# Tile loads of an attention stage: the two heads of a pair on alternate partitions instead of on two halves

## The chip, the core and the metric

The kernel runs on one core of one Trainium2 chip. The metric is the device time of one execution in microseconds. The kernel before took 518.98 us (median of three runs: 518.98, 525.2, 514.63); its profiled execution took 520.31 us, of which the profile's span covers 518.5 us.

## The reference

Attention over chunks, followed by a mixture of experts to which tokens are assigned greedily by gate score with a capacity:

```python
# attention: q, k, v (4, 8, 768, 64), mem_k, mem_v (4, 8, 8, 64)
for c in range(24):                       # chunks of 32 queries
    k_full = concat([mem_k, k[left 16 .. own 32 .. right 8]])   # up to 64 keys
    scores = (q_c @ k_full^T) / 8
    a = softmax(scores)                   # maximum subtracted, sum + 1e-9
    out_c = a @ v_full
# experts: x = attention's output as (3072, 512)
logits = x @ w_gate                       # (3072, 8)
# pairs (token, expert) in falling order of logit; a token takes the first
# expert that has room, each expert takes 384 tokens
for e in range(8):
    h = relu(x[mask_e] @ w1[e])           # (384, 1024)
    out[mask_e] = h @ w2[e]               # (384, 512)
```

All inputs and outputs are float32.

## The kernel before

**Stages.** First comes attention, then the routing of the first expert, then the eight experts with their products, with the routing and the weight preparation of later experts woven in. The change touches attention and one helper that prepares constants.

**Tiles of attention.** The work is cut into 24 tiles. A tile holds one batch, four chunks of 32 queries, and all 8 heads. The heads go in four pairs. A matmul contracts over 128 partitions, and two heads of 64 dimensions share them: the queries `q` of a tile have both heads of a pair stacked over the partitions, and the keys are stored as two blocks, one of which is zero where the other head's dimensions lie. So one matmul with the keys of both blocks gives the scores of both heads, with no mixing. The same trick is used for the values: `s["v"]` are blocks with data on one head's partitions and zeros on the other's.

**The buffers.** Five buffers `kvb` (`NB`) of 128 partitions rotate over the tiles. The columns of each are, in order, `o0`, `v0`, `k0`, `q`, `k1`, `v1`, `o1`, `end` (class `LAY`): odd-chunk values, even-chunk values and keys of head 0, the queries of both, then keys and values of head 1. In the kernel before, head 0 of a pair lies on partitions 0 to 63 and head 1 on 64 to 127. The zero blocks are written once at the start (L69 to L75), since the loads never write to them: data and zeros lie on different partitions.

**The loads.** `load(i)` issues a tile's transfers on SP's queue. The values of even and odd chunks share their first 32 of 64 rows; these rows are loaded once (`cut`) and copied on the chip by `shared(i)`: on GpSimd for head 0 (L128) and on ScalarE for head 1 (L129). Tile 0 is loaded in six transfers, every other tile in four.

**The order of work.** It is written out by hand: in step `t` of a loop over tiles the list `steps` (L231) calls `scores(t)`, `softmax(t)`, `shared(t-1)`, `ptrans(t-1)`, `xtrans(t-3)`, `av(t-2)`, `norm(t-2)`, `rows(t-3)`, `logits2(t-5)` and `logits(t-4)`, and then `load(t+3)`. Each engine takes its instructions in this order. `scores` is 16 matmuls into PSUM (four column groups of 32 at a time); `softmax` is a maximum and a subtraction on VectorE and an exponential on ScalarE; `ptrans` transposes the weights on TensorE; `av` is the product with the values; `rows` scales a tile's rows on GpSimd and stores them to the scratch tensor `xs` in DRAM, through buffers `xr`. `load(t+3)` writes the buffer that `av(t-2)` has read, and SP waits for that.

**Constants.** The generator `constants` (L733) is advanced one step at each tile from the fifth on. Its first step issues the load of the table `cc` on ScalarE's queue and, right behind, casts on GpSimd that read it; later steps fill the tile `io` piece by piece.

Of the kernel before, what the change touches and what calls it, by code (L numbers as in the profile page):

```python
# [11 lines left out]
F32 = mybir.dt.float32  # L12
# [48 lines left out]
def attention(g):  # L61
# [6 lines left out]
    nc.vector.memset(g.zero, 0.0)  # L68
    for i in range(NB):  # L69

        (nc.vector if i < 3 else nc.gpsimd).memset(kvb[i][0:64, L.q + DM:], 0.0)
        if i % 2 == 0:
            nc.scalar.activation(kvb[i][64:P, 0:L.q], g.zero[64:P].to_broadcast([64, L.q]), AF.Copy)
        else:
            nc.gpsimd.memset(kvb[i][64:P, 0:L.q], 0.0)  # L75
    make_identity(nc, g.ident)
# [6 lines left out]

    def load(i):
        kv = kvb[i % NB]

        full = slice(0, L.q + DM), slice(L.q, L.end)
        cut = slice(L.v0, L.q + DM), slice(L.q, L.o1)
        if i == 0:
            first = slice(L.k0, L.q + DM), slice(L.q, L.v1)  # L90
            own = slice(L.v0, L.k0), slice(L.v1, L.o1)
            parts = (0, 64, first), (0, 64, own), (32, 64, (slice(0, L.v0), slice(L.o1, L.end)))
        else:
            parts = (0, 32, cut), (32, 64, full)
        for r0, r1, part in parts:
            for hf, c in enumerate(part):
                r = slice(64 * hf + r0, 64 * hf + r1)
                nc.sync.dma_start(kv[r, c], g.kv[i, r, c.start - L.q * hf:c.stop - L.q * hf])
        st[i] = dict(q=kv[:, L.q:L.q + DM].rearrange("p (r c n) -> p r c n", r=4, c=4), kv=kv,
                     k=blocks(kv, L.k0, L.k1, KW).rearrange("p a (m t n) -> p a m t n", t=3, n=32),  # L100
                     v=[blocks(kv, a, b, VW).rearrange("p a (m n) -> p a m n", n=D + 1)
                        for a, b in ((L.v0, L.v1), (L.o0, L.o1))])

    def scores(i):
        s = st[i]
        ps = pp.tile([P, H, NK], F32, tag="A", name="ps_s")
        for pr in range(4):
            for c in range(4):
                o = ps[32 * c:32 * c + 32, 2 * pr:2 * pr + 2, :]
                nc.tensor.matmul(o.rearrange("p a (t n) -> p a t n", t=2),  # L110
                                 s["q"][:, pr, c, :], s["k"][:, :, 2 * pr + c // 2, 0:2 + c % 2:1 + c % 2],
                                 start=True, stop=True, tile_position=(0, 32 * c))
        s["s"] = ps

    def softmax(i):
        s = st[i]
        ps = s["s"]
        mx = ab.tile([P, H], F32, tag="mx", name="mx", bufs=2)
        nc.vector.tensor_reduce(mx, ps, axis=AX.X, op=ALU.max)
        sub = ab.tile([P, H, NK], F32, tag="sub", name="sub", bufs=2)  # L120
        nc.vector.tensor_tensor(sub, ps, mx.unsqueeze(2).to_broadcast([P, H, NK]), op=ALU.subtract)  # L121
        pe = ab.tile([P, H * NK], F32, tag="pexp", name="pexp", bufs=2)
        nc.scalar.activation(pe, sub.rearrange("p h n -> p (h n)"), AF.Exp, scale=scale)  # L123
        s["p"] = pe

    def shared(i):
        kv = st[i]["kv"]
        nc.gpsimd.tensor_copy(kv[0:32, L.o0:L.v0], kv[0:32, L.v0:L.k0])  # L128
        nc.scalar.activation(kv[64:96, L.o1:L.end], kv[64:96, L.v1:L.o1], AF.Copy)  # L129

# [47 lines left out]
    def rows(i):  # L178
        s = st[i]
        finish(s["pow2"])  # L180
        sx = s["pr"]
        xr = ab.tile([P, XW], F32, tag="xr", name="xr", bufs=2)
        nc.gpsimd.tensor_tensor(xr[:, 0:DM], s["x"], sx[:, 0].to_broadcast([P, DM]), op=ALU.mult)  # L183
        nc.gpsimd.tensor_copy(xr[:, DM:DM + 1], sx[:, 1])
        nc.gpsimd.dma_start(g.xs[i * P:(i + 1) * P, 0:DM + 1], xr[:, 0:DM + 1])
# [42 lines left out]
    def keys(i):  # L228
        finish(first_keys(g, i - 3, i + 1))

    steps = [(scores, 0), (softmax, 0), (shared, 1), (ptrans, 1), (xtrans, 3), (av, 2), (norm, 2), (rows, 3),  # L231
             (logits2, 5), (logits, 4)]
    n = NT - 1
    for t in range(n):
# [6 lines left out]
        yield  # L241
    for f, i in ((scores, n), (shared, n - 1), (ptrans, n - 1), (softmax, n), (shared, n), (xtrans, n - 3),
                 (av, n - 2), (ptrans, n), (logits, n - 4), (rows, n - 3), (av, n - 1), (av, n), (logits2, n - 4),
                 (early, 0), (xtrans, n - 2), (logits, n - 3), (xtrans, n - 1), (logits, n - 2), (early, 1),
                 (xtrans, n), (logits, n - 1), (logits, n), (early, 2), (logits2, n), (hist, 0), (keys, n)):
        f(i)
# [486 lines left out]
def constants(g, consts):  # L733
# [239 lines left out]
def layout(q, k, v, mem_k, mem_v, moe_w_gate, moe_w1, moe_w2):  # L973
# [11 lines left out]
    def order(outside):  # L985
# [38 lines left out]
```

## Time and profile before

| | |
|---|---|
| median of three runs | 518.98 us |
| profiled execution | 520.31 us |
| span of its profile | 518.5 us |
| TensorE busy | 424.6 us (82%) |
| VectorE busy | 315.2 us (61%) |
| ScalarE busy | 329.8 us (64%) |
| GpSimd busy | 253.8 us (49%) |
| first score matmul, last tile's score matmuls | 6.31 us, 121.01 us |
| moved by DMA | 78.87 MB, mean 152 GB/s |

How to read it: busy times are of instructions on the engine; "waited for" tells what ended an idle time; the DMA share is the mean busy share of the core's 16 DMA engines; the clock is the share of TensorE's full clock that was granted. In rows of waits the columns are the total in microseconds, the number of times, and the longest. The page's slices are 13 us wide, so the first nine cover attention.

### The profile page before, as it was taken

Reading aid. Unit: us, or ns where it says so; the run is one execution under the profiler, and the core shown is the slowest. Engines: PE = TensorE matmul, PEld = TensorE weight load, DVE = VectorE, ACT = ScalarE, POOL = GpSimd, SP = SyncE. Lnnn points to the kernel's source line nnn. Section 1 sums busy time; section 2 is a strip of 40 time slices with the busy share of each in tenths; the row PEclk is TensorE's granted clock in tenths of the full one; section 3 lists DMA queues with packets and bytes.
Section 4 is the critical chain, followed back from the end, with each engine's and each line's share of the span. In section 5 each row is a group of like instructions: output and inputs, shape, how many; then the busy total and the mean of one; then the engine's idle time right before and its main releaser. Section 6 shows DMA issues by size and latency. Waiting matters only on the chain.

```text
span 518.5 us, 11009 instructions
## 1 busy us (share of the span) xinstructions
PE 424.6 (82%) x4140; PEld 259.9 (50%) x4140; DVE 315.2 (61%) x1140; ACT 329.8 (64%) x515; POOL 253.8 (49%) x264
## 2 busy tenths in 40 slices
PE   2669677888334686988999999999999999999993
PEld 1447556667232453444555555555555555654641
DVE  4445554655878376775787777787787876423220
ACT  5546664766303857566789578668858956999810
POOL 6145554555122504425638536735825814965821
PEclk9988997999756698697999999999999999999998
DMA  8989999992018200910371290091083069611001
GB/s 214 244 205 272 275 277 267 260 315 101 0 63 296 90 2 1 367 59 21 125 283 41 61 346 20 26 368 55 22 291 136 22 213 362 199 61 40 21 22 40
DMA packets 20150, 78.87 MB, mean 152 GB/s; under 512 B 3776, under 2 KB 3904, under 8 KB 18624
## 3 DMA queue, kind: packets, MB, share of 16 engines
q1 hardware_dynamic: 14048, 58.88, 36.8%
q0 software_dynamic: 5760, 18.90, 10.1%
q8 instruction: 33, 0.54, 0.4%
q10 hardware_dynamic: 288, 0.37, 0.3%
q14 instruction: 21, 0.17, 0.1%
HBM read 65.54 MB, written 12.60 MB: 151 GB/s over the span
## 4 chain that ended last, share of the span: by engine, by line
PE 52%; DVE 16%; DMA 14%; ACT 8%; issue 6%; POOL 2%; SPq 1%; POOLq 0%; DVEq 0%; ACTq 0%
PE ps_hid L684 19%; PE ps_y L703 18%; DMA kvb<-in_kv_dram 13%; PE D L513 3%; PE D L365 2%; PE ps_xg L660 2%; PE ps_av L150 2%; PE ps_s L110 2%; DMA cc<-in_consts_dram 2%; DVE hl L692 2%; ACT hh L691 2%; DVE oa L352 1%; ACT xh L663 1%; DVE xl L666 1%; ACT w1f L602 1%
## 5 line engine op out<-in xcount | busy, mean ns | idle before, releaser
L605 POOL TENSOR_TENSOR w2l<-w2f,w2h 128x1024 f16<-128x1024 f32 x32 | 67.9, 2130 | 35.7 <-ACT w2h L604 35.7
L605 POOL TENSOR_TENSOR w1l<-w1f,w1h 128x1024 f16<-128x1024 f32 (+1 forms) x33 | 68.3, 2075 | 28.7 <-ACT w1h L604 22.4
L684 PEld LDWEIGHTS <-w1h 128*128 128x128 f16 x512 | 48.0, 99 | 33.2 <-issue 4.8
L692 DVE SCALAR_TENSOR_TENSOR hl<-ps_hid,hh 128x384 f16<-128x384 f32 x64 | 35.1, 555 | 42.3 <-ACT hh L691 41.5
L590 POOL DMA_INDIRECT xg<-xs,ids x24 | 23.0, 960 | 72.8 <-DVE R L310 35.7
L703 PEld LDWEIGHTS <-hh 128*128 128x128 f16 x384 | 36.4, 99 | 41.4 <-issue 4.2
L691 ACT ACTIVATE hh<-ps_hid 128x384 f16<-128x384 f32 x64 | 31.1, 486 | 41.0 <-PE ps_hid L684 40.9
L684 PE MATMUL ps_hid<-xh,w1h 128*128 128x384 f16 x256 | 53.5, 332 | 2.4 <-ACT xh L663 2.4
L615 ACT ACTIVATE jk<-w1f 128x1024 f16<-128x1024 f32 x32 | 33.8, 1056 | 33.0 <-DMA w1f<-in_w_dram 31.8
L110 PE MATMUL ps_s<-kvb 128*32 128x128 f32 x768 | 29.3, 293 | 30.8 <-DMA kvb<-in_kv_dram 28.1
L183 POOL TENSOR_TENSOR xr<-x,sxp 128x512 f32<-128x512 f32 x24 | 24.9, 1036 | 59.6 <-DVE sxp L549 23.4
L684 PE MATMUL ps_hid<-xl,w1h 128*128 128x384 f16 x256 | 53.6, 333 | 0.0
L684 PE MATMUL ps_hid<-xh,w1l 128*128 128x384 f16 x256 | 53.1, 331 | 0.0
L703 PE MATMUL ps_y<-w2h,hh 128*128 128x512 f16 x192 | 47.7, 386 | 3.5 <-ACT w2h L604 3.5
L703 PE MATMUL ps_y<-w2h,hl 128*128 128x512 f16 x192 | 50.5, 389 | 0.0
L703 PE MATMUL ps_y<-w2l,hh 128*128 128x512 f16 x192 | 49.7, 389 | 0.0
L716 POOL DMA_INDIRECT out_dram<-y,ids x24 | 23.8, 994 | 43.0 <-DVE y L709 31.2
L123 ACT ACTIVATE pexp<-sub 128x512 f32<-128x512 f32 x24 | 15.1, 630 | 42.2 <-DVE sub L121 42.2
L110 PEld LDWEIGHTS ps_s<-kvb 128*32 128x32 f32 x768 | 22.6, 117 | 34.8 <-issue 34.4
L602 ACT ACTIVATE w1f<-w1f,s1s 128x1024 f32<-128x1024 f32 (+1 forms) x33 | 36.8, 1114 | 0.9 <-ACT s1s L566 0.4
L615 ACT ACTIVATE jk<-w2f 128x1024 f16<-128x1024 f32 x32 | 33.8, 1056 | 5.0 <-DMA w2f<-in_w_dram 2.7
L602 ACT ACTIVATE w2f<-w2f,s2s 128x1024 f32<-128x1024 f32 x32 | 36.5, 1139 | 0.0
(174 smaller groups left out, 855.5 us busy)
## 6 DMA issues: line engine op xcount, KB each, us to landing
w1f<-in_w_dram SPq DMA_DIRECT2D x32, 512.0 KB, 5.7
w2f<-in_w_dram SPq DMA_DIRECT2D x32, 512.0 KB, 8.3
kvb<-in_kv_dram SPq DMA_DIRECT2D x46, 290.0 KB, 8.3
kvb<-in_kv_dram SPq DMA_DIRECT2D x46, 225.0 KB, 7.1
xs<-xr POOLq DMA_DIRECT2D x24, 256.5 KB, 7.5
kvb<-in_kv_dram SPq DMA_DIRECT2D x2, 320.0 KB, 4.4
xg<-xs,ids POOLq DMA_INDIRECT x24, 5.3
out_dram<-y,ids POOLq DMA_INDIRECT x24, 2.8
```

The lines of the kernel that those rows point to most:

```text
L110: nc.tensor.matmul(o.rearrange("p a (t n) -> p a t n", t=2), s["q"][:, pr, c, :], s["k"][:, :, 2 * pr + c // 2, 0:2 + c % 2:1 + c % 2], st ...
L183: nc.gpsimd.tensor_tensor(xr[:, 0:DM], s["x"], sx[:, 0].to_broadcast([P, DM]), op=ALU.mult)
L513: nc.tensor.matmul(ps4, oh[:, :, i], ri[:, i].rearrange("p a b -> p (a b)"), start=(i == 0), stop=(i == NT - 1))
L590: nc.gpsimd.indirect_dma_start(out=xg[a], out_offset=None, in_=g.xs, in_offset=bass.IndirectOffsetOnAxis(ap=ids[:, a:a + 1], axis=0))
L602: nc.scalar.activation(f, f, AF.Copy, scale=s[:, 0:1])
L605: nc.gpsimd.tensor_tensor(l, f, h, op=ALU.subtract)
L615: g.nc.scalar.activation(jk, st[k]["f" + n][j], AF.Abs, accum_out=am[:, j:j + 1])
L684: nc.tensor.matmul(ph[:, 0:CAP], w[:, f // 2, kc, (f % 2) * P:(f % 2) * P + P], x[:, kc, :], start=(n == 0), stop=(n == 3 * KC - 1))
L691: nc.scalar.activation(hh[:, f], ph[:, 0:CAP], AF.Relu)
L692: nc.vector.scalar_tensor_tensor(hl[:, f], ph[:, 0:CAP], 0.0, hh[:, f], op0=ALU.max, op1=ALU.subtract)
L703: nc.tensor.matmul(py, h[:, f, t], w[:, f, :], start=(n == 0), stop=(n == 3 * FC - 1))
L716: sc = g.nc.gpsimd.indirect_dma_start(out=g.out, in_=y, in_offset=None, out_offset=bass.IndirectOffsetOnAxis(ap=ids, axis=0))
```

## The change

The data in DRAM and in the buffers are put in another order. Head 0 of a pair takes the even partitions and head 1 the odd ones, so a tile's transfer for one head goes to 64 partitions with a step of 2 (`kv[hf:P:2, c]`). A tile is loaded in two transfers of 64 rows, tile 0 in four. The rows that even and odd chunks share are stored and loaded twice; `shared` is gone. [...] Scores are written with the two heads alternating, (key, head) instead of (head, key), so that transposed weights have the heads on alternate partitions as well; the matmul's output and the maximum's input have a step of two words. `constants` pauses for five tiles after it has issued the load of the table and three fills, and only then uses the table. `xr` has three buffers instead of two.

```diff
-    for i in range(NB):
-        (nc.vector if i < 3 else nc.gpsimd).memset(kvb[i][0:64, L.q + DM:], 0.0)
-        if i % 2 == 0:
-            nc.scalar.activation(kvb[i][64:P, 0:L.q], g.zero[64:P].to_broadcast([64, L.q]), AF.Copy)
-        else:
-            nc.gpsimd.memset(kvb[i][64:P, 0:L.q], 0.0)
+    nc.gpsimd.memset(kvb[0][:, L.k1:L.v1], 0.0)
+    nc.vector.memset(kvb[0][:, L.k0:L.q], 0.0)
+    nc.vector.memset(kvb[0][:, 0:L.k0], 0.0)
+    nc.gpsimd.memset(kvb[0][:, L.v1:L.end], 0.0)
+    for i in range(1, NB):
+        for r, e in ((slice(0, L.q), i), (slice(L.k1, L.end), i + 1)):
+            if e % 3 == 1:
+                nc.scalar.activation(kvb[i][:, r], g.zero.to_broadcast([P, L.q]), AF.Copy)
+            else:
+                (nc.vector if e % 3 == 0 else nc.gpsimd).memset(kvb[i][:, r], 0.0)
...
     def load(i):
         kv = kvb[i % NB]
-        full = slice(0, L.q + DM), slice(L.q, L.end)
-        cut = slice(L.v0, L.q + DM), slice(L.q, L.o1)
+        parts = [(slice(0, L.k1), slice(L.q, L.end))]
         if i == 0:
-            first = slice(L.k0, L.q + DM), slice(L.q, L.v1)
-            own = slice(L.v0, L.k0), slice(L.v1, L.o1)
-            parts = (0, 64, first), (0, 64, own), (32, 64, (slice(0, L.v0), slice(L.o1, L.end)))
-        else:
-            parts = (0, 32, cut), (32, 64, full)
-        for r0, r1, part in parts:
+            parts = [(slice(L.k0, L.k1), slice(L.q, L.v1)), (slice(0, L.k0), slice(L.v1, L.end))]
+        for part in parts:
             for hf, c in enumerate(part):
-                r = slice(64 * hf + r0, 64 * hf + r1)
-                nc.sync.dma_start(kv[r, c], g.kv[i, r, c.start - L.q * hf:c.stop - L.q * hf])
+                nc.sync.dma_start(kv[hf:P:2, c], g.kv[i, hf, :, c.start - L.q * hf:c.stop - L.q * hf])
...
-        ps = pp.tile([P, H, NK], F32, tag="A", name="ps_s")
+        ps = pp.tile([P, 4, NK, 2], F32, tag="A", name="ps_s")
         for pr in range(4):
             for c in range(4):
-                o = ps[32 * c:32 * c + 32, 2 * pr:2 * pr + 2, :]
-                nc.tensor.matmul(o.rearrange("p a (t n) -> p a t n", t=2),
-                                 s["q"][:, pr, c, :], s["k"][:, :, 2 * pr + c // 2, 0:2 + c % 2:1 + c % 2],
+                o = ps[32 * c:32 * c + 32, pr].rearrange("p (t n) a -> p a t n", t=2)
+                nc.tensor.matmul(o, s["q"][:, pr, c, :], s["k"][:, :, 2 * pr + c // 2, 0:2 + c % 2:1 + c % 2],
                                  start=True, stop=True, tile_position=(0, 32 * c))
...
-        nc.vector.tensor_reduce(mx, ps, axis=AX.X, op=ALU.max)
+        nc.vector.tensor_reduce(mx, ps.rearrange("p r n a -> p r a n"), axis=AX.X, op=ALU.max)
...
-    def shared(i):
-        kv = st[i]["kv"]
-        nc.gpsimd.tensor_copy(kv[0:32, L.o0:L.v0], kv[0:32, L.v0:L.k0])
-        nc.scalar.activation(kv[64:96, L.o1:L.end], kv[64:96, L.v1:L.o1], AF.Copy)
...
-        xr = ab.tile([P, XW], F32, tag="xr", name="xr", bufs=2)
+        xr = ab.tile([P, XW], F32, tag="xr", name="xr", bufs=3)
...
     for t, x in ((g.ones, 1.0), (g.one_row, 1.0), (g.esum, 28.0)):
         nc.gpsimd.memset(t, x)
+    for _ in range(5):
+        yield
     g.e8 = c["e8"]
```

The start of SP's queue before, which holds only the tile loads there (a row is line, operation, buffer and source, partitions x columns, how many; the number behind `kvb` names the buffer):

```order
L98 DMA kvb_88<-in_kv_dram 64x1280 x2
L98 DMA kvb_88<-in_kv_dram 64x520 x2
L98 DMA kvb_88<-in_kv_dram 32x520 x2
L98 DMA kvb_89<-in_kv_dram 32x1800 x2
L98 DMA kvb_89<-in_kv_dram 32x2320 x2
```

The same place now, with what each transfer waits for (the end of a memset on VectorE, GpSimd or ScalarE; DMAHW is an earlier transfer's landing):

```order
L96 DMA kvb_88<-in_kv_dram 64x1280 [waits DVE_49]
L96 DMA kvb_88<-in_kv_dram 64x1280 [waits Pool_49]
L96 DMA kvb_88<-in_kv_dram 64x1040 [waits DVE_49]
L96 DMA kvb_88<-in_kv_dram 64x1040 [waits Pool_49]
L96 DMA kvb_89<-in_kv_dram 64x2320 [waits Activation_49]
L96 DMA kvb_89<-in_kv_dram 64x2320 [waits Pool_49]
```

Tile 1 takes two transfers instead of four, and each buffer's first transfers stand behind a memset.

GpSimd's queue before, from the scaled rows of the first tile on (`xr`, `xs`) to the next value copy:

```order
L128 COPY kvb_90<-kvb_90 32x520
L183 TENSOR_TENSOR xr<-x,sxp 128x512
L184 COPY xr<-sxp 128x1
L185 DMA xs<-xr 128x513
L744 MEMSET ones 128x128
L744 MEMSET one_row 1x128
L744 MEMSET esum 128x1
L749 CAST c_upper<-cc 128x128
```

And now:

```order
L175 TENSOR_TENSOR xr<-x,sxp 128x512
L176 COPY xr<-sxp 128x1
L177 DMA xs<-xr 128x513
L736 MEMSET ones 128x128
L736 MEMSET one_row 1x128
L736 MEMSET esum 128x1
L175 TENSOR_TENSOR xr<-x,sxp 128x512
L176 COPY xr<-sxp 128x1
L177 DMA xs<-xr 128x513
```

Behind the first tile's rows stood the casts, which read the table that was being loaded, and behind these the copies of later tiles' values; now the rows of the next tiles follow, the casts come five tiles later, and no copy of values is left on this engine.

More of the change, by code (lines that the diff above doesn't have):

```diff
@@ L85, in load @@
         kv = kvb[i % NB]
-        full = slice(0, L.q + DM), slice(L.q, L.end)
-        cut = slice(L.v0, L.q + DM), slice(L.q, L.o1)
+        parts = [(slice(0, L.k1), slice(L.q, L.end))]
         if i == 0:
-            first = slice(L.k0, L.q + DM), slice(L.q, L.v1)
-            own = slice(L.v0, L.k0), slice(L.v1, L.o1)
-            parts = (0, 64, first), (0, 64, own), (32, 64, (slice(0, L.v0), slice(L.o1, L.end)))
-        else:
-            parts = (0, 32, cut), (32, 64, full)
-        for r0, r1, part in parts:
+            parts = [(slice(L.k0, L.k1), slice(L.q, L.v1)), (slice(0, L.k0), slice(L.v1, L.end))]
+        for part in parts:
             for hf, c in enumerate(part):
-                r = slice(64 * hf + r0, 64 * hf + r1)
-                nc.sync.dma_start(kv[r, c], g.kv[i, r, c.start - L.q * hf:c.stop - L.q * hf])
-        st[i] = dict(q=kv[:, L.q:L.q + DM].rearrange("p (r c n) -> p r c n", r=4, c=4), kv=kv,
+                nc.sync.dma_start(kv[hf:P:2, c], g.kv[i, hf, :, c.start - L.q * hf:c.stop - L.q * hf])
+        st[i] = dict(q=kv[:, L.q:L.k1].rearrange("p (r c n) -> p r c n", r=4, c=4),
                      k=blocks(kv, L.k0, L.k1, KW).rearrange("p a (m t n) -> p a m t n", t=3, n=32),
@@ L117, in softmax @@
         ps = s["s"]
[L118 to L121, printed above, removed]
+        mx = ab.tile([P, 4, 2], F32, tag="mx", name="mx", bufs=2)
+        nc.vector.tensor_reduce(mx, ps.rearrange("p r n a -> p r a n"), axis=AX.X, op=ALU.max)
+        sub = ab.tile([P, 4, NK, 2], F32, tag="sub", name="sub", bufs=2)
+        nc.vector.tensor_tensor(sub, ps, mx.unsqueeze(2).to_broadcast([P, 4, NK, 2]), op=ALU.subtract)
         pe = ab.tile([P, H * NK], F32, tag="pexp", name="pexp", bufs=2)
-        nc.scalar.activation(pe, sub.rearrange("p h n -> p (h n)"), AF.Exp, scale=scale)
+        nc.scalar.activation(pe, sub.rearrange("p r n a -> p (r n a)"), AF.Exp, scale=scale)
         s["p"] = pe
-    def shared(i):
-        kv = st[i]["kv"]
-        nc.gpsimd.tensor_copy(kv[0:32, L.o0:L.v0], kv[0:32, L.v0:L.k0])
-        nc.scalar.activation(kv[64:96, L.o1:L.end], kv[64:96, L.v1:L.o1], AF.Copy)
     def ptrans(i):
@@ L229, in keys @@
         finish(first_keys(g, i - 3, i + 1))
-    steps = [(scores, 0), (softmax, 0), (shared, 1), (ptrans, 1), (xtrans, 3), (av, 2), (norm, 2), (rows, 3),
+    steps = [(scores, 0), (softmax, 0), (ptrans, 1), (xtrans, 3), (av, 2), (norm, 2), (rows, 3),
              (logits2, 5), (logits, 4)]
@@ L241, in attention @@
         yield
-    for f, i in ((scores, n), (shared, n - 1), (ptrans, n - 1), (softmax, n), (shared, n), (xtrans, n - 3),
+    for f, i in ((scores, n), (ptrans, n - 1), (softmax, n), (xtrans, n - 3),
                  (av, n - 2), (ptrans, n), (logits, n - 4), (rows, n - 3), (av, n - 1), (av, n), (logits2, n - 4),
@@ L998, in layout @@
     rows = np.stack([np.concatenate([vo[:, 0], ve[:, 0], kl[:, 0], ql[:, 0]], 2),
-                     np.concatenate([ql[:, 1], kl[:, 1], ve[:, 1], vo[:, 1]], 2)], 1).reshape(NT, P, -1)
+                     np.concatenate([ql[:, 1], kl[:, 1], ve[:, 1], vo[:, 1]], 2)], 1).reshape(NT, 2, 64, -1)
     wg = np.zeros((P, KC, 32), np.float32)
```

## The prediction

> **What bounds the kernel now.** I read the page first, then busy time by stage, then who waits for whom in the first 125 us, then the order of time at a few tiles. The page, with its traffic rows and its DMA issues (KB each, microseconds to landing):
>
> ```profile
> span 518.5 us, 11009 instructions
> ...
> DMA  8989999992018200910371290091083069611001
> GB/s 214 244 205 272 275 277 267 260 315 101 0 63 296 90 2 1 367 59 21 125 283 41 61 346 20 26 368 55 22 291 136 22 213 362 199 61 40 21 22 40
> ...
> w1f<-in_w_dram SPq DMA_DIRECT2D x32, 512.0 KB, 5.7
> ...
> kvb<-in_kv_dram SPq DMA_DIRECT2D x46, 290.0 KB, 8.3
> kvb<-in_kv_dram SPq DMA_DIRECT2D x46, 225.0 KB, 7.1
> xs<-xr POOLq DMA_DIRECT2D x24, 256.5 KB, 7.5
> kvb<-in_kv_dram SPq DMA_DIRECT2D x2, 320.0 KB, 4.4
> ```
>
> The span is cut into slices of 13 us. In the first nine, which are attention, the DMA engines are full while they move only 205 to 315 GB/s; later slices with weight loads reach 367. So in attention the engines are busy, yet each is slow. Busy time in stretches of the program sets a rate beside each share (the last columns are clock, DMA share, GB/s):
>
> ```profile
> core 0: us, PE busy (x) PEld busy (x) DVE busy (x) ACT busy (x) POOL busy (x), PEclk, DMA share, GB/s
> 6.30:26.00 19.70, 10.75 (x208) 8.32 (x208) 8.11 (x19) 8.48 (x14) 4.37 (x8) 1.00 1.03 247
> 39.00:121.00 82.00, 64.78 (x1348) 51.49 (x1344) 43.74 (x151) 51.40 (x105) 42.75 (x76) 0.91 0.97 269
> ...
> 121.00:131.00 10.00, 7.81 (x189) 6.42 (x181) 6.14 (x24) 7.62 (x15) 5.17 (x9) 1.00 0.23 82
> 131.00:518.50 387.50, 333.30 (x2251) 187.35 (x2251) 247.01 (x922) 251.72 (x370) 189.58 (x146) 0.91 0.34 122
> 212.00:217.00 5.00, 5.00 (x34) 2.81 (x34) 2.85 (x10) 4.03 (x7) 1.95 (x3) 0.50 1.01 391
> ```
>
> Full engines carry 391 GB/s of weights (512 KB each over 128 partitions), but 247 GB/s where almost nothing but `kvb` loads moves, and 269 GB/s where `xs` stores are mixed in. A `kvb` load covers 32 neighbouring partitions. The waits of the first 125 us (total, times, longest) say who pays:
>
> ```profile
> DVE mx L119 <- PE ps_s L110: 31.3, 18, 4.5
> PE ps_s L110 <- DMA kvb<-in_kv_dram: 28.1, 16, 6.3
> ...
> POOL c_upper L749 <- DMA cc<-in_consts_dram: 6.2, 1, 6.2
> ...
> PE ps_av L150 <- POOL kvb L128: 2.7, 1, 2.7
> ```
>
> The score matmuls wait for loads, and VectorE's maximum waits for the score matmuls. In order of time, the first scores, those of three tiles in the middle, and the last tile's:
>
> ```profile
> 6.31 1.08 PE L110 MATMUL ps_s<-kvb 128*32 128x128 f32 x16 [6.31 <-DMA kvb<-in_kv_dram]
> ...
> 90.90 1.05 PE L110 MATMUL ps_s<-kvb 128*32 128x128 f32 x32
> ...
> 94.19 1.08 PE L110 MATMUL ps_s<-kvb 128*32 128x128 f32 x32
> ...
> 97.59 1.07 PE L110 MATMUL ps_s<-kvb 128*32 128x128 f32 x31
> ...
> 121.01 1.05 PE L110 MATMUL ps_s<-kvb 128*32 128x128 f32 x32
> ```
>
> From first to last tile: (121.01 - 6.31) / 23 = 4.99 us a tile. A tile now loads 2 x (290 + 225) = 1030 KB = 1.055 MB and stores 256.5 KB = 0.263 MB, together 1.318 MB; at 269 GB/s that is 4.90 us. So the DMA alone explains the pace. After a stall, when two tiles' data were there already, the pace was 94.19 - 90.90 = 3.29 and 97.59 - 94.19 = 3.40 us: that is what the other engines can do. TensorE's busy time in 39 to 121 us, which holds 17 tiles, is 64.78 / 17 = 3.81 us a tile at a mean clock of 0.91, with the logits' matmuls; I take 3.8 as its floor.
>
> **The loads.** Each tile becomes two transfers of 64 x 2320 x 4 B = 580 KB: 1160 KB = 1.188 MB, 13% more than 1.055. With the stores, 1.451 MB a tile. At which rate? No transfer of the trace goes to alternate partitions, so I bound it. From below, the rate of today's mixture, 269 GB/s: 5.39 us a tile. From above, the weights' 391 GB/s, which reach all 128 partitions: 3.71 us. The break-even with 4.99 us lies at 1.451 / 4.99 = 291 GB/s. A transfer on partitions 0, 2, ... 126 is like the weights' in that it reaches the whole height of the memory at once, and like the old one in its source, one contiguous block with rows of 9280 B. I take the upper row, because in today's mixture the engines are full at both rates and what differs most between the two kinds is the partitions that one transfer touches.
>
> [...]
>
> **The pace after.** DMA 3.71 and TensorE 3.8 are nearly equal, and each tile's load may be issued only when a buffer comes free, as today:
>
> ```profile
> SPq L98 <- PE ps_av L150: 50.4, 18, 6.9
> ```
>
> Two limits this close never overlap perfectly; I add 0.2 us to the larger and take 4.0 us a tile. The last score then starts 23 x 4.0 = 92 us after the first.
>
> **The zeroing and the first load.** Today no load waits for a memset, because data and zeros lie on different partitions. Now whole columns are zeroed first, and the loads wait:
>
> ```profile
> 0.76 1.60 POOL L75 MEMSET kvb<- 64x1808 f32 x1 [0.29 <-POOLq L1013]
> 0.77 6.21 SPq L98 DMA_DIRECT2D kvb<-in_kv_dram  x11
> ...
> 1.24 1.56 DVE L71 MEMSET kvb<- 64x1808 f32 x1 [0.34 <-issue]
> ...
> 2.46 4.90 ACT L73 ACTIVATE kvb<-zero 64x1808 f32<-64x1808 f32 x3
> ```
>
> VectorE's first memset is now 768 columns on 128 partitions instead of 1808 on 64; if its time goes by the columns, 1.56 x 768 / 1808 = 0.66 us, done at 1.24 + 0.66 = 1.90 instead of the issue at 0.77: +1.1 us. Everything queued on SP stands behind it. The first pair of 320 KB (0.655 MB) moves in 1.7 us at 391 instead of 2.65 at 247: -1.0. Bounds for the first score: 6.0 to 7.4 us; I take 6.4. Tile 1's load waits for a ScalarE write, which ends at 2.46 + 1.63 = 4.1 (a third of 4.90), and then lands about 4.1 + 1.188 / 0.391 + 1.75 (the 4.4 us of the first loads less the 2.65 they moved) = 8.9, ahead of the next scores at 6.4 + 4.0 = 10.4. So nothing more.
>
> **The shared copies.** POOL and ACT each lose one copy a tile; which wait goes with them?
>
> ```profile
> L128 POOL COPY kvb<-kvb x24: 606/624/630, 7.8 to 124.4; 32x520 f32<-32x520 f32 x24
> L129 ACT ACTIVATE kvb<-kvb x24: 632/632/635, 16.3 to 125.9; 32x520 f32<-32x520 f32 x24
> ```
>
> ACT was busy 51.40 of 82 us and POOL 42.75 in the steady stretch, so 0.62 and 0.63 us a tile are off the path there; in the last tiles, with no load outstanding, up to 0.6 us once. I count zero. One wait does go: the value product of tile 3 stood behind a copy that stood behind the constants.
>
> ```profile
> 33.45 0.29 POOL L749 CAST c_upper<-cc 128x128 bf16<-128x128 f32 x1 [6.19 <-DMA cc<-in_consts_dram]
> ...
> 35.76 1.70 PE L150 MATMUL ps_av<-kvb,pt 128*32 128x130 f32 x30 [2.72 <-POOL kvb L128]
> ```
>
> In that stretch the DMA fell idle, since no buffer came free:
>
> ```profile
> 26.00:39.00 13.00, 8.01 (x160) 6.28 (x164) 5.68 (x22) 5.48 (x11) 6.36 (x20) 0.89 0.83 206
> ```
>
> (1 - 0.83) x 13 = 2.2 us, gone in either case, since no `kvb` copy is left on POOL and the constants are used five tiles later. It is contained in the 4.99, so it enters the sum only where the old pace is scaled. The third `xr` buffer concerns POOL alone, which has 82 - 42.75 = 39 us idle.
>
> **The score matmuls.** They now write every second word of PSUM. Today's cost and VectorE's read of the same tile:
>
> ```profile
> L110 PE MATMUL ps_s<-kvb 128*32 128x128 f32 x536 | 19.6, 282 | 13.2 <-DMA kvb<-in_kv_dram 10.5 <-issue 2.6
> ...
> L119 DVE TENSOR_REDUCE mx<-ps_s 128x8 f32<-128x512 f32 x17 | 11.7, 690 | 19.3 <-PE ps_s L110 19.3
> ```
>
> No matmul of this trace writes with a step. A tile's 32 passes run in 1.05 us, four column groups at once, so 128 words per group take 1.05 / 8 = 131 ns, about one word a nanosecond. Products of the expert stage (on the chain of waits, 12 of them in a row) write faster:
>
> ```profile
> 257.08 2.59 PE ps_y L703 x12
> ```
>
> 2.59 / 12 = 216 ns for 512 words (the group's shape, 128x512), 2.4 a nanosecond. A write that used half of each access would still keep up with one word a nanosecond, so I count nothing; the ceiling, twice the time, is +1.1 us a tile (a rival below). VectorE's maximum now reads with a step: its 690 ns for 512 words is 0.74 words a nanosecond, slower than either, and I leave it.
>
> **The sum.** First score 6.4 + 23 x 4.0 = 98.4 against 121.0: -22.6 us. Behind the last tile nothing changes: 121 to 131 (DMA share 0.23) and 131 to 518.5 are the same instructions, and they start when attention ends. The profiled run took 520.3 us, span and what lies around it, 1.3 above the median of 519.0: 520.3 - 22.6 = 497.7, about 498 us.
>
> **Rivals.**
>
> *The rate stays, and the kernel is slower.* The loads may not be slow for the partitions that one transfer covers. Each engine may take a run of neighbouring rows, and pairs of engines may meet on the same place as now, or the contiguous source may be the brake. For it: nothing in the trace shows which engine writes which row, and the source stays as it is. Against it: the gap between 247 and 391 at full engines. Price: with `kvb` alone at 247, 1.188 / 0.247 = 4.81 us, and the stores take their own share of the engines,
>
> ```profile
> q0 software_dynamic: 1360, 4.47, 17.0%
> ```
>
> 17% of 82 us for 17 tiles, 0.82 us: together 5.63 us a tile. 6.4 + 23 x 5.63 = 135.9, less 2.2 for the stall at the constants, is 133.7 against 121.0: +12.7, 533 us. At 269 for the mixture it is 6.4 + 23 x 5.39 - 2.2 = 128.2: +7.2, 527.5. It decides below 291 GB/s. Chance 0.20: 0.13 at the slower end, 0.07 within 2%.
>
> *Half of the gain.* Rows of 9280 B through alternate partitions share some of the conflict: 320 GB/s, the middle between 247 and 391. 1.451 / 0.320 = 4.53 us, 6.4 + 104.2 = 110.6: -10.4, 510 us. Chance 0.12, split evenly by the 2% line.
>
> *The step in PSUM costs.* Score matmuls of twice the time make TensorE 3.8 + 1.1 = 4.9 us a tile; with 0.2 on top 5.1, 6.4 + 117.3 = 123.7: about +2.7, 523 us, with the DMA idle for a fifth of the time. Against it speak the words per nanosecond above; the trace has no such write. Chance 0.06. [...]
>
> **How the numbers follow.** The forecast has the remaining 0.62. Its own range: the fastest pace seen, 3.4 us a tile, cannot hold for logits tiles; 3.5 gives 6.4 + 80.5 = 86.9, -34, 486 us. If TensorE and DMA overlap badly, 4.5 us gives 109.9, -11, 509 us. The range of all cases goes from 486 up to 527, the milder end of the first rival, and leaves out the 0.13 above and some 0.05 below. Two per cent, about 10 us, is what a measurement of this kernel can tell from no change; its three runs lay 514.6 to 525.2. Faster by more than 2%: 0.60 of the forecast and 0.06 of the half gain, 0.66. Slower by more: 0.13. Within: 0.21.
>
> **What would show it.** In the profile after, the stretch of attention should read above 340 GB/s at a full DMA share, or a DMA share well under 1; `kvb` landings from issue should fall under 7 us for 580 KB; the last score should start near 98 us; PE's idle time before the scores "<-DMA kvb" should fall from 28.1 to under 10 us, and TensorE should be busy 9 tenths in slices 2 to 7. If the rate is still near 250 at share 1, the first rival is right. If the mean of a score matmul goes from 282 ns far up, or 32 of them take 2 us at full clock, the third is. If the first score starts after 7.4 us, the zeroing was priced too low. The expert stage should take the same 387 us behind the end of attention; a change there of more than 4 us would mean that something is tied to attention that I have not seen.

## The result and the profile after

The changed kernel took 502.06 us (median of four runs, 500.35 to 504.13) beside 518.47 us of the kernel before: a ratio of 0.971, with a 95% interval of 0.963 to 0.979. It is faster by about 3%. The profiled execution took 500.35 us with a span of 498.1 us, against 520.31 and 518.5, so it gained 20.0 us; the medians gained 16.4 us.

The page of the kernel after, span, TensorE and traffic in slices of 12.5 us, the score matmuls, and two rows of the DMA issues (KB each, microseconds to landing):

```profile
span 498.1 us, 10862 instructions
...
PE   1978888882357859989999999999999999999992
...
DMA  7999999911090009102800920550280098601001
GB/s 265 378 335 334 330 381 342 352 69 43 28 378 18 2 3 372 68 23 82 340 24 23 347 97 23 209 234 23 85 338 22 22 340 302 214 12 43 22 22 42
...
L108 PE MATMUL ps_s<-kvb 128*32 128x128 f32 x768 | 28.5, 288 | 18.2 <-DMA kvb<-in_kv_dram 17.8
...
kvb<-in_kv_dram SPq DMA_DIRECT2D x46, 580.0 KB, 7.0
w1f<-in_w_dram SPq DMA_DIRECT2D x32, 512.0 KB, 5.7
```

The DMA engines are as full as before in attention, but the first eight slices now read 265 to 381 GB/s, where the nine of before read 205 to 315, and attention ends a slice earlier. A `kvb` transfer of 580 KB lands in 7.0 us; one of 290 KB took 8.3.

Busy time in stretches of the kernel after (the last columns are granted clock, DMA share, GB/s); the third row is steady attention, the last one everything from 10 us behind the last tile's scores:

```profile
6.30:26.00 19.70, 15.01 (x315) 11.95 (x307) 10.90 (x29) 9.09 (x17) 4.62 (x11) 1.00 0.98 372
26.00:39.00 13.00, 9.91 (x235) 7.91 (x237) 7.32 (x26) 6.46 (x15) 4.29 (x8) 1.00 0.98 349
39.00:98.00 59.00, 49.99 (x1129) 40.54 (x1120) 37.32 (x135) 33.21 (x74) 30.05 (x60) 0.97 0.99 348
...
110.70:498.10 387.40, 333.00 (x2241) 186.79 (x2241) 245.58 (x918) 250.75 (x369) 189.59 (x146) 0.91 0.33 122
```

Before, the first row read 247 GB/s at a share of 1.03, the steady one 269 at 0.97, and 26 to 39 us had a share of 0.83. The expert stage takes 387.4 us, before 387.5: the whole difference lies in attention. In order of time, what the first load waits for, and the scores of the first two tiles, of one tile in the middle and of the last:

```profile
1.03 0.70 DVE L71 MEMSET kvb<- 128x768 f32 x1
...
1.76 6.62 SPq L96 DMA_DIRECT2D kvb<-in_kv_dram  x9
...
5.93 1.93 PE L108 MATMUL ps_s<-kvb 128*32 128x128 f32 x32 [5.93 <-DMA kvb<-in_kv_dram]
...
12.03 1.94 PE L108 MATMUL ps_s<-kvb 128*32 128x128 f32 x32 [4.16 <-DMA kvb<-in_kv_dram]
...
38.48 1.08 PE L108 MATMUL ps_s<-kvb 128*32 128x128 f32 x32
...
100.70 1.45 PE L108 MATMUL ps_s<-kvb 128*32 128x128 f32 x32 [0.30 <-DMA kvb<-in_kv_dram]
```

The last scores start at 100.70 us instead of 121.01, which is 20.3 us earlier, and that is the gain of the profiled execution (20.0). The mean pace is (100.70 - 5.93) / 23 = 4.12 us a tile. From tile 8, at 38.48, fifteen tiles take 4.15 us each. Waits of the kernel after in its first 125 us, and those on SP's queue in the first 110 us (total, times, longest):

```profile
PE ps_s L108 <- DMA kvb<-in_kv_dram: 17.8, 12, 5.9
...
DVE mx L116 <- PE ps_s L108: 16.2, 16, 4.7
```

```profile
SPq L96 <- PE ps_av L142: 43.1, 15, 6.0
SPq L96 <- PE D L204: 15.6, 4, 4.5
SPq L96 <- DMA cc<-in_consts_dram: 1.3, 1, 1.3
```

TensorE still waits for loads, less: 17.8 us instead of 28.1, and 5.9 of it is the first tile. VectorE's wait for scores halves, from 31.3 to 16.2.

### The profile page after: what moved, and what is told of

Read it like the earlier page. It is cut to its first block, busy times and chain, and to the rows that moved or that the text cites. A ratio compares the mean times of both kernels' runs of the same rounds, so it can differ in the third digit from the quotient of the medians.

```text
span 498.1 us, 10862 instructions
## 1 busy us (share of the span) xinstructions
PE 419.7 (84%) x4140; PEld 256.4 (51%) x4140; DVE 314.9 (63%) x1141; ACT 311.9 (63%) x491; POOL 239.5 (48%) x241
## 4 chain that ended last, share of the span: by engine, by line
PE 58%; DVE 16%; DMA 10%; ACT 7%; issue 6%; POOL 2%; SPq 0%; POOLq 0%; DVEq 0%; ACTq 0%
PE ps_hid L676 20%; PE ps_y L695 18%; DMA kvb<-in_kv_dram 10%; PE ps_s L108 3%; PE ps_av L142 3%; PE D L505 3%; PE D L357 2%; PE ps_xg L652 2%; PE ps_pt L127 2%; DVE hl L684 2%; ACT hh L683 2%; DVE oa L344 2%; ACT xh L655 1%; DVE xl L658 1%; ACT w1f L594 1%
## 5 line engine op out<-in xcount | busy, mean ns | idle before, releaser
L108 PE MATMUL ps_s<-kvb 128*32 128x128 f32 x768 | 28.5, 288 | 18.2 <-DMA kvb<-in_kv_dram 17.8
L701 DVE TENSOR_SCALAR y<-ps_y,inv,xg 128x512 f32<-128x512 f32 x24 | 19.4, 807 | 26.4 <-PE ps_y L695 23.6
```

Of the source, the lines that this page charges most:

```text
L108: nc.tensor.matmul(o, s["q"][:, pr, c, :], s["k"][:, :, 2 * pr + c // 2, 0:2 + c % 2:1 + c % 2], start=True, stop=True, tile_position=(0, ...
L701: nc.vector.tensor_scalar(y, py, s["inv"], s["xg"][a][:, DM:DM + 1], op0=ALU.mult, op1=ALU.mult)
```

## The experiments

The theory after this look: in this kernel a tile load is fast when one transfer reaches both halves of the partitions (372 GB/s in the first stretch), and slow when it stays in one half (247 before). Its rivals: that fewer and larger transfers, the zeroing, the pause or the third `xr` buffer did it. The DMA alone still sets the pace, or it shares it with TensorE. All ratios below are to the kernel before.

**The loads on halves again.** Everything else of the change stays: the same two transfers of 580 KB, the zeroing, the pause. Only the partitions go back to halves, and the scores with them to their old layout.

```diff
-                nc.sync.dma_start(kv[hf:P:2, c], g.kv[i, hf, :, ...])
+                nc.sync.dma_start(kv[64 * hf:64 * hf + 64, c], g.kv[i, hf, :, ...])
...
-                o = ps[32 * c:32 * c + 32, pr].rearrange("p (t n) a -> p a t n", t=2)
+                o = ps[32 * c:32 * c + 32, pr].rearrange("p a (t n) -> p a t n", t=2)
```

> The changed kernel with one thing undone: head 0 of a pair lies on partitions 0 to 63 again and head 1 on 64 to 127 (scores written head by head to match); two transfers of 580 KB a tile, the same bytes, source rows, zeroing, constants and buffers as in the changed kernel. Theory (the partitions that one transfer covers set its rate): the rate falls back to 240 to 270 GB/s at a full DMA share, 5.4 to 5.6 us a tile, last score at 128 to 134 us, time 525 to 535 us, slower than the kernel before. Rival (fewer and larger transfers, or more bytes in flight, made the gain): it stays at 500 to 505 us with packets of 9280 B at 349 ns.

Measured: 539.19 us (537.65 to 540.29), ratio 1.047, interval 1.038 to 1.056. Stretches of this run, and its first and last scores:

```profile
6.30:26.00 19.70, 10.05 (x147) 7.63 (x151) 4.98 (x10) 3.94 (x6) 1.17 (x3) 1.00 1.03 226
...
39.00:98.00 59.00, 40.76 (x789) 31.95 (x788) 27.76 (x99) 24.53 (x54) 22.10 (x46) 0.88 1.02 260
```

```profile
7.36 1.03 PE L108 MATMUL ps_s<-kvb 128*32 128x128 f32 x13 [7.36 <-DMA kvb<-in_kv_dram]
...
137.94 1.08 PE L108 MATMUL ps_s<-kvb 128*32 128x128 f32 x32 [1.52 <-DMA kvb<-in_kv_dram]
```

The DMA engines are full and move 226 GB/s where almost only loads run; with the loads on alternate partitions the same stretch has 372. One changed index, with the layout of the scores that it brings, is worth 37 us (539.19 against 502.06). So the rest of the change, without it, makes the kernel slower: it loads 13% more bytes at no more than the old rate (226 GB/s against 247 in the first stretch, 260 against 269 in the steady one). The traces also hold the time of every packet, and a row of 9280 B is one packet: between 39 and 98 us the median packet of a load takes 629 ns on halves and 349 ns in the changed kernel. The time lies above the expectation, and so does the pace, 5.68 us a tile against 5.4 to 5.6; the prediction's first rival had 5.63 (below).

**Is it the step, or the reach?** The loads go to every second partition, but each transfer stays in one half: 32 rows to 0 to 63 and 32 rows to 64 to 127.

```diff
-                nc.sync.dma_start(kv[hf:P:2, c], g.kv[i, hf, :, ...])
+                for r in (0, 64):
+                    nc.sync.dma_start(kv[r + hf:r + 64:2, c],
+                                      g.kv[i, hf, r // 2:r // 2 + 32, ...])
```

> The changed kernel with each transfer cut by rows into two: 32 rows on every second partition of 0 to 63, then 32 rows on every second partition of 64 to 127 (290 KB each, four a tile). Heads still alternate, bytes are the same; only the reach of one transfer is half the height. Theory (the reach counts, not the alternation): 220 to 260 GB/s at a full DMA share, 525 to 540 us as with the two halves. Rival (neighbouring partitions within a transfer are the brake, the step of 2 cures it): 500 to 506 us.

Measured: 535.45 us (533.41 to 537.31), ratio 1.037, interval 1.029 to 1.045.

```profile
6.30:26.00 19.70, 10.55 (x172) 8.20 (x173) 5.77 (x11) 4.66 (x8) 1.17 (x3) 1.00 1.00 240
...
39.00:98.00 59.00, 40.54 (x798) 32.64 (x791) 27.14 (x98) 24.58 (x55) 22.11 (x46) 0.86 1.00 267
```

With the step and without the reach the rate is 240 GB/s, near the 226 of halves and far from 372. Here the reach of one transfer decides, not the alternation. This run has four transfers a tile, so it alone doesn't exclude their number; the run on halves had the same two as the changed kernel, and was slow. A transfer of 32 rows over both halves was not run; it would show whether the size of a transfer counts beside its reach.

**Scores written without a step.** The matmuls write PSUM contiguously, and VectorE's subtraction reads with the step instead.

```diff
-                o = ps[32 * c:32 * c + 32, pr].rearrange("p (t n) a -> p a t n", t=2)
+                o = ps[32 * c:32 * c + 32, pr].rearrange("p a (t n) -> p a t n", t=2)
...
-        nc.vector.tensor_tensor(sub, ps, mx...)
+        nc.vector.tensor_tensor(sub, ps.rearrange("p r a n -> p r n a"), mx...)
```

> The changed kernel with the score matmuls writing PSUM without a step (head by head), and VectorE's subtraction reading PSUM with a step instead. Theory (the step in PSUM costs nothing): mean of a score matmul and of the subtraction unchanged (288 and 692 ns within 3%), time 502 us within 1%. Rival (the step slows the matmuls): up to 1.1 us a tile comes back, 480 to 495 us.

Measured: 501.73 us (499.81 to 504.47), ratio 0.972, interval 0.964 to 0.981: no different from the changed kernel. Groups by form between 39 and 98 us (busy, mean ns | idle), first of this run and then of the kernel after:

```profile
L108 PE MATMUL ps_s<-kvb 128*32 128x128 f32 x448 | 15.9, 285 | 6.7 <-DMA kvb<-in_kv_dram 6.7
...
L118 DVE TENSOR_TENSOR sub<-ps_s,mx 128x512 f32<-128x512 f32 x14 | 9.7, 692 | 0.5
```

```profile
L108 PE MATMUL ps_s<-kvb 128*32 128x128 f32 x469 | 15.9, 274 | 5.9 <-DMA kvb<-in_kv_dram 5.6
...
L118 DVE TENSOR_TENSOR sub<-ps_s,mx 128x512 f32<-128x512 f32 x14 | 9.7, 691 | 0.5
L116 DVE TENSOR_REDUCE mx<-ps_s 128x8 f32<-128x512 f32 x14 | 9.7, 690 | 7.3 <-PE ps_s L108 7.3
```

Writing with a step of two words cost TensorE nothing here (274 ns with it, 285 without, at a granted clock of 0.97 and 0.94), and neither VectorE's maximum (690 ns with it and without) nor its subtraction (692 with it, 691 without) had a price for it.

**Fewer bytes.** The values of tiles 5 to 23 aren't loaded.

```diff
+        if i > 4:
+            parts = [(slice(L.k0, L.k1), slice(L.q, L.v1))]
```

> The changed kernel, but the values of tiles 5 to 23 are left out of the loads (only keys and queries, 640 KB a tile; the values of an earlier tile are used). It shows the pace without the DMA's limit: 0.655 + 0.263 = 0.918 MB a tile is 2.4 us at 391 GB/s. Theory (DMA and TensorE limit together): 3.5 to 3.7 us a tile, last score at 88 to 92 us instead of 101, time 488 to 492 us. Rival (TensorE alone sets the 4.12 us): no change, 500 us.

Measured: 491.49 us in one run. Its steady stretch, and its scores of tile 8 and of the last tile:

```profile
39.00:98.00 59.00, 55.82 (x1338) 46.50 (x1332) 43.22 (x157) 38.85 (x87) 35.48 (x69) 1.00 0.79 231
```

```profile
38.72 1.06 PE L110 MATMUL ps_s<-kvb 128*32 128x128 f32 x32
...
91.67 1.17 PE L110 MATMUL ps_s<-kvb 128*32 128x128 f32 x32
```

The DMA share falls to 0.79, TensorE is busy 55.82 of 59 us, and fifteen tiles take (91.67 - 38.72) / 15 = 3.53 us each. That is close to TensorE's own pace at a clock of 1.00. The changed kernel's 4.15 us lies 0.6 us above it, its DMA engines are full, and with fewer bytes it gets faster; so the loads still set most of the steady pace after the change. Its 1.451 MB at 348 GB/s are 4.17 us, but that is the same measurement read another way, since the rate was taken from this stretch.

The packets in the changed kernel's trace say more. Between 39 and 98 us three of four load packets take 349 to 354 ns, the others longer, and the mean is 426 ns. If all took 349 ns, and the 64 packets of a tile's stores their median of 160, a tile would take (128 x 349 + 64 x 160) / 16 = 3.43 us on the 16 engines, as an estimate. What slows the fourth packet was not tried.

**The pauses and the third buffer alone.** They are put into the kernel before.

```diff
-        xr = ab.tile([P, XW], F32, tag="xr", name="xr", bufs=2)
+        xr = ab.tile([P, XW], F32, tag="xr", name="xr", bufs=3)
...
+    for _ in range(5):
+        yield
     g.e8 = c["e8"]
```

> The kernel before with only the side parts of the change: five pauses before the constants are used and a third xr buffer; loads on two halves as before. Theory: the idle DMA at 26 to 39 us goes, 2.2 us, so 515 to 518 us, within noise of the kernel before. Rival (the side parts carry much of the gain): 505 to 510 us.

Measured: 517.85 us (514.33 to 521.82), ratio 1.007, interval 1.002 to 1.011: no gain. The DMA share between 26 and 39 us stayed low, though no value product stood behind the constants any more:

```profile
26.00:39.00 13.00, 8.15 (x144) 6.44 (x144) 5.16 (x18) 7.18 (x15) 6.61 (x15) 0.80 0.81 196
```

Waits on SP's queue, in the kernel before (first 130 us) and in this run (20 to 40 us), say why:

```profile
SPq L98 <- DMA cc<-in_consts_dram: 8.0, 1, 8.0
```

```profile
SPq L98 <- DMA cc<-in_consts_dram: 8.7, 1, 8.7
```

A tile load, which has nothing to do with the constants' table, waited 8 us for its landing. The program's instructions tell how that comes about. This is SP's queue and the table's issue on ScalarE's in the kernel before, each with the earlier landing it waits for:

```order
L98 DMA kvb_92<-in_kv_dram 32x2320 [waits DMAHW5_49]
L98 DMA kvb_92<-in_kv_dram 32x2320 [waits DMAHW7_49]
...
L98 DMA kvb_89<-in_kv_dram 32x1800 [waits DMAHW5_49,Activation_49]
L98 DMA kvb_89<-in_kv_dram 32x2320 [waits DMAHW6_49]
...
L737 DMA cc<-in_consts_dram 128x600 [waits DMAHW6_49]
```

In the program's instructions the transfers of SP and ScalarE take eight completion counters (DMAHW0 to 7) in turn; in the trace of the kernel before, the 100 that the two issue in the first 125 us use eight. The table, issued at 25.41 us, took number 6 in its turn and landed at 33.40; the next tile load that got number 6 was issued at 33.42, and everything behind it on SP came later still.

**The same with the table on another queue.** In the program's instructions GpSimd's transfers take other counters (DMASW0 to 7); in the trace of the kernel before, its row stores use eight that no transfer of SP or ScalarE uses.

```diff
-    nc.scalar.dma_start(cc, consts)
+    nc.gpsimd.dma_start(cc, consts)
```

> The kernel before with the five pauses and the third xr buffer, as in the run of the side parts, and besides with the constants' table issued on GpSimd's queue instead of ScalarE's. My theory: the DMA engines idled between 26 and 39 us because the tile loads and the table shared one row of eight completion counters, so that one tile load on SP had to wait 8.0 to 8.7 us until the table had landed. On GpSimd's queue the table takes no such counter. Then SP shows no wait for cc, the DMA share between 26 and 39 us goes from 0.81 to 0.95 or more, the last tile's scores come about 2 us earlier, and the time is about 516, which is within the noise of the kernel before. Rival: the loads stop there for another reason (a buffer that comes free late); then SP waits for something else in that stretch and the DMA share stays near 0.81.

Measured: 514.33 us (510.78 to 517.26), ratio 0.991, interval 0.986 to 0.995. SP has no wait for `cc` left, and the stretch reads:

```profile
26.00:39.00 13.00, 10.56 (x200) 8.40 (x204) 6.23 (x20) 7.23 (x15) 6.26 (x15) 0.87 1.02 248
```

```profile
117.42 1.08 PE L110 MATMUL ps_s<-kvb 128*32 128x128 f32 x32 [1.85 <-DMA kvb<-in_kv_dram]
```

The DMA share is 1.02 instead of 0.81, so the theory of the counters holds for the idle DMA engines. What that is worth in time the traces don't show. The last scores start 3.6 us before those of the kernel before, but 2.5 us after those of the run with the side parts alone, whose profiled execution was the fastest of its ten:

```profile
114.89 1.08 PE L110 MATMUL ps_s<-kvb 128*32 128x128 f32 x32 [0.28 <-DMA kvb<-in_kv_dram]
```

Over all executions the two runs differ by 3.5 us in their medians and by 1.6% in their ratios, and each lies within 2% of the kernel before.

**The changed kernel without the pause.**

```diff
-    for _ in range(5):
-        yield
     g.e8 = c["e8"]
```

> The changed kernel without the pause of five tiles: GpSimd's casts stand right behind the issue of the table again and wait for it, 6.2 us in the kernel before. My theory: no value product of the changed kernel waits for a copy on GpSimd, so that nothing but the rows' stores stands behind the casts, and the third xr buffer and GpSimd's idle time cover them: 500 to 504 us, ratio to the kernel before 0.966 to 0.976, last scores within 1.5 us of 100.7. Rival: the pause is part of the gain; then the stores come late, the time is 3 us or more above that of the changed kernel, and TensorE waits behind GpSimd's rows.

Measured: 508.28 us (506.78 to 510.1), ratio 0.981, interval 0.972 to 0.990; the rival's side. Here the two stops come together. VectorE and TensorE of this run in order of time, and its stretch:

```profile
34.24 0.23 DVE L757 COPY R<-pairs 128x64 int32<-128x64 int32 x1 [7.76 <-POOL pairs L753]
```

```profile
37.51 1.12 PE L127 MATMUL ps_pt<-ident,pexp 128*128 128x128 f32 x4 [5.94 <-ACT pt L129]
```

```profile
26.00:39.00 13.00, 5.52 (x111) 4.64 (x104) 4.82 (x18) 3.56 (x9) 5.33 (x17) 0.84 0.79 288
```

`constants`, one step behind its casts, has VectorE copy `pairs`. Without the pause that copy waits 7.76 us for GpSimd, which waits for the table; behind it on VectorE stand the maximum and the subtraction of a tile, and TensorE's transposes wait 5.94 us for what follows from them. Not the rows' stores, as the rival had it, but the softmax stood behind the casts. The same copy in the kernel before:

```profile
35.17 0.23 DVE L765 COPY R<-pairs 128x64 int32<-128x64 int32 x1 [4.43 <-POOL pairs L761]
```

It waited 4.43 us there. The last scores of the run without the pause start at 108.55 us, 7.9 later than with it.

**A sixth buffer.**

```diff
-    NB, L = 5, LAY
+    NB, L = 6, LAY
```

> The changed kernel with six tile buffers instead of five, so that a load waits for the value product of one tile earlier. [...] Theory (DMA and TensorE still limit each other through the buffers): pace from 4.1 to 3.8 us a tile, -7 us, 494 to 497 us. Rival (the DMA's own rate is the limit): 500 to 503 us.

Measured: 499.15 us (498.95 to 502.64), ratio 0.967, interval 0.961 to 0.973; last scores at 98.95. That can't be told from the changed kernel. SP waits less for buffers and more for the table:

```profile
SPq L96 <- PE ps_av L142: 30.2, 13, 5.2
SPq L96 <- PE D L204: 14.3, 3, 5.0
SPq L96 <- DMA cc<-in_consts_dram: 5.8, 1, 5.8
```

**Shared rows loaded once again.** The alternating layout stays; the values that even and odd chunks share are loaded once and copied on the chip as in the kernel before, with five and with six buffers.

```diff
-        parts = [(slice(0, L.k1), slice(L.q, L.end))]
+        parts = [(slice(L.v0, L.k1), slice(L.q, L.o1))]
...
+        for hf, c in enumerate((slice(L.o0, L.v0), slice(L.o1, L.end))):
+            nc.sync.dma_start(kv[64 + hf:P:2, c], g.kv[i, hf, 32:64, ...])
...
+        nc.gpsimd.tensor_copy(kv[0:64, L.o0:L.v0], kv[0:64, L.v0:L.k0])
+        nc.scalar.activation(kv[0:64, L.o1:L.end], kv[0:64, L.v1:L.o1], AF.Copy)
```

> The changed kernel with the shared values loaded once again and copied on the chip (GpSimd and ScalarE, 64 partitions x 520 each a tile): two transfers of 450 KB on all partitions and two of 65 KB on the upper half. Bytes a tile fall from 1.451 to 1.318 MB with the stores. Theory (DMA still limits half of the time): -0.36 us a tile at most, 494 to 499 us. Rival (the copies put a new wait before the value products, or the small transfers cost as much as they save): 502 to 508 us.

> Both: six tile buffers, and shared values loaded once and copied. Theory (two separate shares of the same limit): 488 to 493 us, close to the 491 us of the kernel that leaves most values out. Rival (TensorE's 3.2 to 3.5 us a tile and its stalls bind first): no better than the better of the two.

Measured: 502.51 us (500.45 to 504.81), ratio 0.973, interval 0.967 to 0.979, with five buffers, and 503.49 us (498.98 to 504.79), ratio 0.972, interval 0.966 to 0.978, with six. No gain in either. The first stretch with five buffers:

```profile
6.30:26.00 19.70, 15.24 (x301) 12.17 (x305) 9.78 (x25) 9.26 (x18) 5.79 (x13) 1.00 0.97 308
```

The bytes saved are given back by the rate: 308 GB/s at a share of 0.97, against 372 at 0.98. Why is not shown. The small transfers that go in addition stay in the upper half, as the slow ones above do; but the large ones, which reach both halves, became slower as well: a packet of 7200 B takes 349 ns on the mean in this stretch, where the changed kernel takes 387 ns for one of 9280 B.

**The table on GpSimd's queue, with six and with five buffers.**

> The changed kernel with six kvb buffers and the constants' table on GpSimd's queue. With six buffers SP waited 5.8 us for the table, and TensorE had one stop of 1 to 2 us for a load behind that. My theory: that stop goes, the DMA share stays above 0.97 through 26 to 39 us, and the last scores come 0.5 to 1.5 us earlier than with six buffers alone (98.95): 497 to 499 us, which three rounds cannot tell from the 499 of six buffers. Rival: TensorE's own work, not the loads, sets the end there already; then the last scores stay within 0.5 us of 98.95.

> The changed kernel with five buffers, as it is, and only the constants' table moved to GpSimd's queue. It splits the gain of the last run (495.28 us, last scores at 96.64) between the sixth buffer and the queue. My theory: with five buffers SP waits for the value product that frees a buffer nearly all the time (43.1 us) and only 1.3 us for the table, so the queue alone gives about 1 us: 500 to 502 us, last scores 99 to 101. Rival: the table's share of the counters cost more than SP's 1.3 us shows, since the loads behind it come late too; then the last scores are at 98 or earlier and the time is 496 to 498.

Measured: 495.28 us (494.07 to 495.96), ratio 0.955, interval 0.947 to 0.963, with six buffers, and 499.77 us (499.29 to 502.06), ratio 0.964, interval 0.957 to 0.971, with five. The last scores start at 96.64 and 99.80 us. With five, SP waits for buffers anyway, as the theory had it (its 500 to 502 us were missed by 0.2). With six the queue gives 2.3 us in the last scores, more than either theory had, from one trace each. The run with six buffers:

```profile
6.30:26.00 19.70, 16.06 (x314) 13.04 (x315) 11.79 (x28) 8.55 (x16) 6.01 (x12) 1.00 1.00 402
26.00:39.00 13.00, 11.37 (x268) 9.53 (x270) 9.01 (x31) 7.88 (x19) 6.52 (x12) 1.00 1.02 386
39.00:98.00 59.00, 50.16 (x1175) 41.11 (x1164) 38.37 (x143) 34.61 (x76) 30.77 (x61) 1.00 0.96 343
```

```profile
PE ps_s L108 <- DMA kvb<-in_kv_dram: 9.9, 2, 6.4
```

Only two score matmuls of the first 125 us still wait for a load, both at the start. This version beats both kernels; its interval lies just below that of the changed kernel.

Even so its pace from tile 8 on is (96.64 - 36.52) / 15 = 4.01 us, and not 3.53. Seven times before the last scores TensorE stands idle for 0.6 to 2.1 us without a wait that the profile names, 9.8 us in all. Each of these stops ends 1.2 to 1.7 us after a 16 KB transfer on the queue that brings instructions (q8 of the profile) has ended. That TensorE waits there for its own instructions, behind full DMA engines, is argued from this and was not tried.

## Why the prediction was right, point by point

**The bound.** Right. The DMA set the pace through its rate; the runs on halves show it from the other side, full engines at 226 GB/s.

**The rate of the new loads.** Right in direction and cause, and mis-sized. I took the weights' 391 GB/s; the steady stretch has 348 at a share of 0.99, between the upper bound and the break-even of 291. So the term of the loads was 4.17 us a tile and not 3.71. TensorE's floor was mis-sized the other way, 3.8 against the measured 3.53; the clock is most of it, since I took the 3.81 from a stretch with a mean clock of 0.91, and the 3.53 were measured at 1.00 (3.81 x 0.91 = 3.47, as an estimate). With 0.2 us for bad overlap, an allowance that no run shows apart, the two errors nearly cancelled, which was luck: 4.0 forecast, 4.12 measured. As measured the two are not "nearly equal", 4.15 and 3.53. With every load packet at the 349 ns that most of them take they would be, 3.43 and 3.53 by the estimate above; so a part of the 0.6 us between them may be the bad overlap that I had put at 0.2, and how much is open. The reason given, that a transfer reaches the whole height of the memory, is what the runs on halves and of the half-reaching step bear out: 226 and 240 GB/s in the first stretch, where the changed kernel has 372.

**The start.** The first memset ended at 1.03 + 0.70 = 1.73 us (1.90 forecast) and the first scores started at 5.93 (6.4, bounds 6.0 to 7.4): priced slightly too high. "So nothing more" for tile 1 failed: its load was to land at 8.9 us, and the scores of tile 1 waited 4.16 us for it, until 12.03. The sum for 8.9 had left out tile 0's second pair of transfers, 2 x 260 KB = 0.532 MB, which stands ahead of tile 1 on SP's queue: 1.4 us at 391 GB/s. The rest of the 3.1 us was not followed up. Tile 1 came 6.10 us behind tile 0 instead of 4.0. The kernel before had the same gap, and I had not looked at the scores of its tile 1:

```profile
12.23 1.94 PE L110 MATMUL ps_s<-kvb 128*32 128x128 f32 x32 [3.98 <-DMA kvb<-in_kv_dram]
```

That is 12.23 - 6.31 = 5.92 us in the trace of before, hidden in its mean of 4.99. The change did not shorten it. Behind tile 1 the pace after is (100.70 - 12.03) / 22 = 4.03.

**The sum.** Last scores at 98.4 forecast, 100.70 measured: -0.5 for the first, +2.1 for the gap to tile 1, +0.7 for 22 tiles at 4.03. The time of the profiled execution is 2.7 us above the 497.7 of the sum: 2.3 from there, and 0.4 behind the last scores (500.35 - 100.70 = 399.65 against 520.31 - 121.01 = 399.30). That execution was the fastest of the four; their median, 502.06, is 4.4 us above the sum.

**The stall at the constants.** "Gone in either case" came true for the changed kernel, where the DMA share between 26 and 39 us rose from 0.83 to 0.98, and not for the kernel before with the pauses, where it was 0.81. The reason that I gave, that no buffer came free, was wrong. The row that I quoted, a value product behind GpSimd's copy, was the last link of another chain. Two waits held that stretch: SP's 8.0 us for the table through the shared counter, and VectorE's 4.4 us for `pairs`. That SP's wait covers VectorE's in the kernel before is argued from the times of all executions: without VectorE's (the pauses and the third buffer) nothing was gained, and without both 0.9%. The single traces of these two runs, with last scores at 114.89 and 117.42 us, don't bear it out. The table on the other queue without the pauses was not run. In the changed kernel SP's wait shrank to 1.3 us, and there the pause is worth 6 us (508.28 against 502.06), far above the 2.2 that I had read from the idle DMA. I had asked what the pause saves beside the old loads, and not what its absence would cost beside faster ones.

**The shared copies and the third buffer.** "Zero" holds for the copies: put back, with the loads they save, they change nothing that can be measured. The third `xr` buffer was run together with the pauses only, without a gain.

**The rivals.** *The rate stays* was refuted for this change, and confirmed in its price by the run on halves: 5.63 us a tile against (137.94 - 7.36) / 23 = 5.68, where 7.36 is the start of its first scores. Its 533 us came out as 537.65 in the profiled execution (median 539.19) mostly since the 2.2 us that I took off for the constants were not to be had, the first scores started 1.0 us later, and the pace was 0.05 slower: together 4.3 of the 4.6. *Half of the gain* assumed 320 GB/s; 348 lies nearer to it than to 391, though the time lies nearer to the forecast, by the two errors above. *The step in PSUM costs* is refuted: 285 ns without the step, 274 with it.

**What would show it.** Above 340 GB/s at a full share: yes. Landings under 7 us: 7.0, not quite. Last scores near 98: 100.7. TensorE's idle time before scores under 10 us: no, 17.8. TensorE busy 9 tenths in slices 2 to 7: no, mostly 8. The last two would have told that the loads still bound the kernel; in the version with six buffers and the other queue the idle time is 9.9. The expert stage within 4 us: yes.

## What to carry to other kernels

Where DMA engines are full and move far less than in another stage (here 247 GB/s against 391), look at which partitions one transfer reaches: spreading each transfer over both halves (502.06 us against 539.19 within halves) was worth more here than the 13% of bytes that were loaded in addition. Read the waits of the queue that issues the loads for names that don't belong there, such as a table that another engine loads. And an idle stretch may be held by two waits at once: taking one away may show nothing until the other is gone too, so price each with the other removed, and over many executions, since the last scores of single traces moved by several us.

## What the hardware did that I had not expected

A transfer of 580 KB to 64 partitions was 1.6 times as fast over both halves as within one (372 against 226 GB/s at full engines), although on halves the two transfers of a tile go to different halves and are issued one behind the other. Why they don't make up for each other was not tried.

With a sixth buffer and the table on GpSimd's queue the rate of the first stretch went above the weights' 391 GB/s, to 402. Between 39 and 98 us it was 343 to 356 with six buffers, 348 after the change: stores of rows run there as well, and 343 came with a share of 0.96. How much of that the stores take was not measured apart.

A load on SP waited 8.0 to 9.4 us for the landing of a table issued on ScalarE's queue, since both took their completion counters from the same eight (with the table on GpSimd's queue SP had no such wait); in the other kernels with the table on that queue it was at most 5.8 us. The 9.4 us are from the run with the step but without the reach:

```profile
SPq L97 <- DMA cc<-in_consts_dram: 9.4, 1, 9.4
```
